# Block means on TensorE and whole rows of keys for the first batch, in a band attention with two gated layers

## The chip, the cores and the metric

One core of a Trainium2 chip runs the kernel. The metric is the device time of one execution in microseconds (us), as a median of several runs. TensorE multiplies matrices, VectorE and ScalarE do element-wise work and reductions, GpSimd does element-wise work too, and SyncE issues the loads. All loads of this kernel stand in SyncE's queue; ScalarE issues the stores and a few copies within on-chip memory.

## The reference

```python
def _attn_ref(q, k, v):                     # 2 batches, 8 heads, 768 rows, 64 columns
    block, window = (32, 16)
    k_sum = k.reshape(B, H, nb, block, D).max(axis=3)
    v_sum = v.reshape(B, H, nb, block, D).mean(axis=3)
    scores_l = scale * np.matmul(q, k.transpose(0, 1, 3, 2))
    mask_l = np.abs(pos[:, None] - pos[None, :]) < window
    scores_s = scale * np.einsum('bhsd,bhnd->bhsn', q, k_sum) + np.log(block)
    scores_all = np.concatenate([np.where(mask_l, scores_l, -1e9), scores_s], axis=-1)
    a = softmax(scores_all)
    return np.matmul(a, np.concatenate([v, v_sum], axis=2))

x = attention as 1536 rows of 512
x = (sigmoid(x @ w_gate) * (x @ w_val)) @ w_out          # 512 -> 1536 -> 512
out = max(x @ w1, x @ w2, x @ w3) @ w_out2               # 512 -> 768 -> 512
```

Each row attends to a band of 31 neighbours and to 24 summaries of blocks of 32 rows: a maximum for the keys, a mean for the values.

## The kernel before

The attention is cut into 16 units: a batch b, a half a of 384 rows, and a pair p of heads. The first eight units are batch 0, units 0 to 3 its first half and units 4 to 7 its second. For one unit, q is loaded with its 128 rows (two heads of 64 columns) on the partitions, and the keys of the unit with the same layout. A tile of 64 queries is scored against 96 neighbouring keys and against the 24 block maxima (L576). VectorE adds the mask and takes the minimum of the negated scores (L583), ScalarE takes exponentials (L589), VectorE normalizes (L594, L595, L598) or, in later units, ScalarE does (L603), TensorE transposes (L608), and a product with the values gives the unit's part of x (L618, "PV").

The keys come in two forms. For units 0 to 3 (`whole`) they are read from `kn`, the whole row of keys of a pair, 768 long with 16 of padding on either side, which is also what the block maxima are taken from (L511). The scores are then two passes, one against windows of `kn` and one against the maxima `ks`. All other units load `kw`, keys laid out in windows of 96 with 24 places behind each; VectorE copies the maxima into these places (L558), and one pass of matmuls does both. There are three buffers for `kn`, two for `kw`, four for `q`, three for `v`.

The block means of v are made once a pair. `vn` holds 96 x 2 x 512 floats: the 32 rows of a block lie on four partitions with eight rows of 64 columns each, for two heads. GpSimd adds the eight rows in three halving steps (L516) into `vr`, one float32 matmul with a constant matrix `avg` adds the four partitions and divides by 32 (L521), ScalarE copies the result out of PSUM (L524) and into the last 24 partitions of the values `vt` (L567, or a DMA at L565 in later units).

The two gated layers behind it use weights that are stored as 64-bit integers; they are loaded in 96 transfers (L392, three buffers `raw`), put together by three VectorE instructions (L399, L404, L408) and split into a high part (ScalarE, L342) and a low part (VectorE, L345). Products with x run in three passes of these parts, 128 x 384 columns a matmul (L697 for the gates and values, L731 for the output product, L821 and L928 in the second layer). The first group of gates and values for batch 0, first half, needs units 0 to 3; its second half needs units 4 to 7.

No engine decides its order while it runs. Each piece of work is a task with an engine, a planned duration, a due time, the tasks it depends on, the buffers it takes and those it uses, and tasks that it must not be planned ahead of (`after`, which orders the plan and adds no wait on the chip). `order` plays the tasks through: for each engine it looks for those that could start first and takes the most pressing by due time, and the instructions are written out in that order. On the chip each engine and the load queue go through this order and wait where something isn't there. Loads are listed as soon as their buffer is free. Until 45 us of the planned time, dummy matmuls on a constant tile (L980) fill TensorE's planned gaps.

Due times of a unit are counted back from its target T: the keys and q by KEYS0 = 14 for units 0 to 3 and KEYS = 24 for others, v by ROWS0 = 2 or ROWS = 4, the rows for the means by SUMS0 = 14 in batch 0 and SUMS = 8 in batch 1.

Of the kernel before, what the change touches and what calls it, by code (L numbers as in the profile page):

```python
# [9 lines left out]
F32 = mybir.dt.float32  # L10
# [30 lines left out]
SLACK = {"PE": 0.05, "DVE": 0.12, "ACT": 0.1, "POOL": 0.0, "SP": 0.0}  # L41
OVER = 0.0
BANKS_H, BANKS_W, BANKS_T = 7, 12, 5
BANKS_KW, BANKS_KN, BANKS_Q, BANKS_V = 2, 3, 4, 3


class Buf:
# [25 lines left out]
class Plan:  # L73
# [11 lines left out]
    def add(self, eng, dur, due, fn, deps=(), new=(), uses=(), after=(), tab=None):  # L85
        t = Task(eng, dur, due, fn, [d for d in deps if d], list(new), list(uses), [d for d in after if d], tab)
        self.tasks.append(t)
        return t
# [114 lines left out]
def kernel(  # L203
# [15 lines left out]
    nc = tc.nc  # L219
    B, NPAIR, _, S = qt.shape  # L220
    D = vw.shape[-1]
    NT, DM = out.shape
    NB = S // BLK
    HALF = S // 2
# [6 lines left out]
    CW = 96 + NB  # L231
# [5 lines left out]
    const = ctx.enter_context(tc.tile_pool(name="const", bufs=1))  # L237
# [7 lines left out]
    ps_m = ctx.enter_context(tc.tile_pool(name="ps_m", bufs=4, space=bass.MemoryType.PSUM))  # L245
    ps_s = ctx.enter_context(tc.tile_pool(name="ps_s", bufs=4, space=bass.MemoryType.PSUM))

    ident = const.tile([128, 128], F32, name="ident")
    masks = const.tile([128, 3, CW], F32, name="masks")
    avg = const.tile([96, 128], F32, name="avg")  # L250

    def build_consts():
        make_identity(nc, ident)
# [27 lines left out]
    add = plan.add  # L281
# [5 lines left out]
    def psum_s(shape):  # L287
        return Buf(ps_s, shape, F32, "s", 4)
# [31 lines left out]
    at = FIRST  # L320
# [152 lines left out]

    att_cm = tc.tile_pool(name="ap", bufs=2)
    ap_ = att_cm.__enter__()
    xt = {(b, a, k): Buf(xp, [128, 2, 2, HALF], F32R, "x", 8) for b in range(B) for a in range(2) for k in range(2)}
    xready = {}
    chain = {}  # L480
# [1 line left out]
    def after(tag, t):  # L482

        p = chain.get(tag)
        if p:
            t.after.append(p)
        chain[tag] = t
        return t

    def load_task(tag, n, shape, src, dur, t):  # L490
        b = Buf(ap_, shape, F32, tag, n)

        def fn(what=tag):
            nc.sync.dma_start(out=b.t[0:src.shape[0]], in_=src)

        return b, after(tag, add("SP", dur, t, fn, new=[b]))

    kblock, vblock = {}, {}
    attention = []

    def make_sums(b, p, T):

        kt, lk = load_task("kn", BANKS_KN, [128, S + 2 * WIN], kn[b, p], 1.14, T - (KEYS if b else KEYS0))
        r, lr = load_task("vn", 2, [96, 2, 8 * D], vn[b, p], 1.092, T - (SUMS if b else SUMS0))
        ks = Buf(ap_, [128, NB], F32, "ks", 4)
        vr = Buf(ap_, [96, 2, D], F32, "vr", 2)
        vs = Buf(ap_, [128, 2 * D], F32, "vs", 4)
        ps = psum_s([128, 2 * D])

        def kmax():  # L510
            nc.vector.tensor_reduce(  # L511
                out=ks.t, in_=kt.t[:, WIN:WIN + S].rearrange("p (n w) -> p n w", w=BLK), axis=AX.X, op=ALU.max)

        def vadd():
            for n in (4, 2, 1):
                nc.gpsimd.tensor_tensor(  # L516
                    out=r.t[:, :, 0:n * D] if n > 1 else vr.t, in0=r.t[:, :, 0:n * D],
                    in1=r.t[:, :, n * D:2 * n * D], op=ALU.add)

        def vmean():  # L520
            nc.tensor.matmul(ps.t, lhsT=avg, rhs=vr.t, start=True, stop=True)  # L521

        def vcopy():
            nc.scalar.activation(out=vs.t, in_=ps.t, func=ACTF.Copy)  # L524

        k = add("DVE", 0.87, T - 13.5, kmax, [lk], [ks], [kt])
        v1 = add("POOL", 2.5, T - 8, vadd, [lr, built], [vr], [r])
        v2 = add("PE", 0.22, T - 5, vmean, [v1], [ps], [vr])
        v3 = add("ACT", 0.2, T - 4.5, vcopy, [v2], [vs], [ps])
        kblock[b, p] = ks, k, kt, lk  # L530
        vblock[b, p] = vs, v3
        attention.extend([k, v1, v2, v3])

    def make_unit(u, i):
        b, p, a = u
        T = target[u]
        if a == 0:
            make_sums(b, p, T)
        whole = i < NPAIR
        ks, kk, kt, lk = kblock[b, p]  # L540
        if not whole:
            kt, lk = load_task("kw", BANKS_KW, [128, TPU, 2, CW], kw[b, p, a], 1.024, T - KEYS)
        q, lq = load_task("q", BANKS_Q, [128, HALF], qt[b, p, :, HALF * a:HALF * a + HALF], 0.546,
                          T - (KEYS0 if whole else KEYS))
        vt, lv = load_task("v", BANKS_V, [CW, TPU, 2, 2, D], vw[b, p, a], 0.82, T - (ROWS0 if whole else ROWS))
# [4 lines left out]
        ps = [psum_s([128, TPU, CW]) for h in range(2)]  # L550
        pa = [(psum_m if i < FREE_M else psum_s)([128, TPU, 128]) for h in range(2)]
        at = [Buf(ap_, [128, TPU, 128], F32, "at", 2) for h in range(2)]
        px = psum_s([128, HALF])
# [7 lines left out]
        def vfill(dma):  # L561
            o = vt.t[96:CW].rearrange("p t par h d -> p (t par) (h d)")
            src = vs.t[96:CW, None, :].to_broadcast([NB, 2 * TPU, 2 * D])
            if dma:
                nc.scalar.dma_start(out=o, in_=src)  # L565
            else:
                nc.scalar.activation(out=o, in_=src, func=ACTF.Copy)  # L567

        def scores(c0, c1):
            for t in range(TPU):  # L570
                for h in range(2):
                    r = slice(64 * h, 64 * h + 64)
                    for par in range(2):
                        c = 128 * t + 64 * par
                        k = kt.t[r, t, par] if not whole else ks.t[r] if c0 else kt.t[r, c:c + 96]
                        nc.tensor.matmul(  # L576
                            ps[h].t[64 * par:64 * par + 64, t, c0:c1], lhsT=q.t[r, c:c + 64], rhs=k,
                            start=True, stop=True)
# [49 lines left out]
        if whole:  # L628
            s0 = after("S", add("PE", 1.25, T - 11, lambda: scores(0, 96), [lk, lq], ps + e + [nm, sm], [q, kt]))
            s1 = add("PE", 0.95, T - 11, lambda: scores(96, CW), [s0, kk], [], [q, ks] + ps)  # L630
            s0.rows, s1.rows = 0.5, 0.25
            attention.append(s0)
        else:
            f1 = add("DVE", 0.23, T - 11.5, fill, [kk, lk], [], [kt, ks])
            s1 = after("S", add("PE", 1.5, T - 11, lambda: scores(0, CW), [f1, lq], ps + e + [nm, sm], [q, kt]))
            s1.rows = 0.45
            attention.append(f1)
        AT = []
# [18 lines left out]
        dma = i >= BY_DMA  # L657
        g1 = add("ACT", 0.12 if dma else 0.83, T - 5, lambda: vfill(dma), [kv], [], [vt, vs], [lv])
        g1.dma = 0.63 if dma else 0.0
        w1 = after("PV", add("PE", 0.95, T, pv, AT + [g1, lv], [px], [vt] + at))  # L660
        key = b, a, p // 2
        first = key not in xstart
        x1 = add("ACT", 0.37, T + 1, xhi, [w1], [x] if first else [], [px] if first else [px, x])
# [279 lines left out]
    built = add("POOL", 5.0, -100.0, build_consts)  # L943
    for i, u in enumerate(units):
        make_unit(u, i)
# [22 lines left out]
    with tc.manual_schedule():  # L968
        idle = const.tile([128, 384], BF16, name="idle")
        nc.vector.memset(idle, 0.0)  # L970
        for t in plan.order():
            for b in t.new:
                b.take()
            if t.idle:
# [3 lines left out]
                n = min(o.shape[1], 384)  # L978
# [62 lines left out]
```

## Time and profile before

| | us |
|---|---|
| median of three runs | 569.16 (568.2 to 570.3) |
| the profiled execution | 567.5 |
| its span, first to last instruction | 565.7 |
| TensorE busy | 545.6 (96%) |
| VectorE busy | 436.3 (77%) |
| ScalarE busy | 291.2 (51%) |
| GpSimd busy | 26.7 (5%) |

The profile is of one execution; its own time stands beside its span, and a median of runs is another number. PE is TensorE's matmuls, PEld its weight loads, DVE VectorE, ACT ScalarE, POOL GpSimd, SPq the load queue. A float32 matmul appears as two records. Busy times of TensorE are of a pipeline, so that a busy engine can still be slow; PEclk is the share of full clock that it was granted.

### The profile page before, as it was taken

What the parts mean: (1) busy time and instruction counts of PE and PEld (TensorE: products, weight loads), DVE (VectorE), ACT (ScalarE), POOL (GpSimd) and SP (SyncE); (2) the same over time, 40 slices, a digit from 0 to 9 for tenths busy, and PEclk for the clock granted to TensorE, in tenths of its full rate; (3) what the DMA queues carried; (4) which work ended last, traced back from release to release, by engine and by line L of the source; (5) the groups of instructions that cost most, each with busy time, mean ns of one, the idle gap of its engine ahead of it and who ended that gap; (6) DMA issues with size and microseconds to landing.
All of it is one profiled execution on the core that took longest, in us unless ns stands there. A gap on an engine that the chain in (4) does not pass through costs nothing.

```text
span 565.7 us, 9849 instructions
## 1 busy us (share of the span) xinstructions
PE 545.6 (96%) x3740; PEld 518.5 (92%) x3740; DVE 436.3 (77%) x995; ACT 291.2 (51%) x665; POOL 26.7 (5%) x42
## 2 busy tenths in 40 slices
PE   7798889999999999999999999999999999999997
PEld 4587779999999999999999999999999999997886
DVE  6998796896897488949996997799999997885000
ACT  3777778678656656966441432435434333453111
POOL 5223300000000000000000000000000000000000
PEclk7979889999999999999999999999999999999999
DMA  8999964565274343520552453130322222000111
GB/s 280 326 259 265 265 206 132 146 229 171 92 235 145 100 106 134 183 80 1 153 193 103 148 158 141 43 108 5 111 82 102 75 75 80 34 0 38 56 75 56
DMA packets 24862, 73.40 MB, mean 130 GB/s; under 512 B 2800, under 2 KB 6256, under 8 KB 24816
## 3 DMA queue, kind: packets, MB, share of 16 engines
q1 hardware_dynamic: 21696, 69.05, 40.4%
q10 hardware_dynamic: 3120, 3.74, 1.9%
q8 instruction: 29, 0.48, 0.3%
q14 instruction: 17, 0.14, 0.1%
HBM read 69.04 MB, written 3.15 MB: 128 GB/s over the span
## 4 chain that ended last, share of the span: by engine, by line
PE 84%; DMA 8%; DVE 5%; ACT 2%; issue 0%; SPq 0%; ACTq 0%; DVEq 0%
PE m L697 31%; PE m L731 17%; PE s L821 11%; PE m L821 11%; PE m L928 9%; DMA raw<-in_wts_dram 4%; DMA kn<-in_kn_dram 3%; DMA v<-in_vw_dram 2%; PE s L618 1%; PE s L608 1%; PE s L576 1%; DVE c L408 1%; DVE c L404 1%; DVE w L345 1%; DVE e L598 0%
## 5 line engine op out<-in xcount | busy, mean ns | idle before, releaser
L697 PE MATMUL m<-x,w 128*128 128x384 f32 x1152 | 212.4, 340 | 0.3 <-ACT t L711 0.3
L697 PEld LDWEIGHTS m<-x,w 128*128 128x128 f32 x1152 | 200.8, 190 | 2.1 <-ACT t L711 0.6
L731 PE MATMUL m<-h,w 128*128 128x384 f32 x576 | 109.1, 341 | 2.4 <-DVE w L345 1.0
L731 PEld LDWEIGHTS m<-h,w 128*128 128x128 f32 x576 | 100.6, 190 | 3.9 <-DVE w L345 1.3
L342 ACT ACTIVATE w<-c 128x512 fp32r<-128x512 f32 x96 | 58.0, 611 | 67.2 <-DVE c L408 43.0
L345 DVE TENSOR_TENSOR w<-c,w 128x512 fp32r<-128x512 f32 x96 | 65.4, 682 | 6.3 <-ACT w L342 6.0
L404 DVE SCALAR_TENSOR_TENSOR c<-raw,c 128x512 int32<-128x512 int32 x96 | 66.3, 691 | 0.6
L408 DVE SCALAR_TENSOR_TENSOR c<-raw,c 128x512 int32<-128x512 int32 x96 | 65.4, 684 | 0.6
L821 PE MATMUL m<-x,w 128*128 128x384 f32 x294 | 56.3, 335 | 1.2 <-ACT t L836 1.2
L821 PE MATMUL s<-f,w 128*128 128x384 f32 x294 | 55.9, 334 | 0.0
L821 PEld LDWEIGHTS m<-x,w 128*128 128x128 f32 x294 | 51.3, 188 | 1.6 <-ACT t L836 1.5
L821 PEld LDWEIGHTS s<-f,w 128*128 128x128 f32 x294 | 51.4, 188 | 0.0
L399 DVE TENSOR_SCALAR c<-raw 128x512 int32<-128x512 int32 x96 | 42.1, 440 | 9.4 <-DMA raw<-in_wts_dram 8.6
L342 ACT ACTIVATE h<-t 128x384 fp32r<-128x384 f32 x48 | 25.0, 522 | 30.5 <-DVE t L716 30.2
L716 DVE TENSOR_TENSOR t<-m,t 128x384 f32<-128x384 f32 x48 | 26.6, 554 | 17.2 <-PE m L697 8.6
L711 ACT ACTIVATE t<-m 128x384 f32<-128x384 f32 x48 | 23.5, 491 | 28.6 <-PE m L697 28.1
L589 ACT ACTIVATE e<-e,nm 128x120 f32<-128x120 f32 x96 | 36.7, 386 | 0.2
L345 DVE TENSOR_TENSOR h<-t,h 128x384 fp32r<-128x384 f32 x48 | 27.5, 576 | 6.7 <-ACT h L342 6.7
L938 ACT ACTIVATE c<-m 128x512 f32<-128x512 f32 (+1 forms) x13 | 7.4, 566 | 40.0 <-PE m L928 39.6
L836 ACT ACTIVATE t<-s 128x384 f32<-128x384 f32 x27 | 13.3, 491 | 24.4 <-PE s L821 24.4
L928 PE MATMUL m<-w,x 128*128 128x512 f32 (+1 forms) x126 | 24.9, 359 | 0.0
L928 PE MATMUL m<-w,f 128*128 128x512 f32 x108 | 24.7, 389 | 0.0
(106 smaller groups left out, 597.2 us busy)
## 6 DMA issues: line engine op xcount, KB each, us to landing
raw<-in_wts_dram SPq DMA_DIRECT2D x96, 512.0 KB, 3.8
v<-in_vw_dram SPq DMA_DIRECT2D x16, 288.0 KB, 4.9
kw<-in_kw_dram SPq DMA_DIRECT2D x12, 360.0 KB, 8.7
kn<-in_kn_dram SPq DMA_DIRECT2D x8, 400.0 KB, 8.8
vn<-in_vn_dram SPq DMA_DIRECT2D x8, 384.0 KB, 9.8
q<-in_qt_dram SPq DMA_DIRECT2D x16, 192.0 KB, 6.3
out_dram<-c ACTq DMA_DIRECT2D x11, 256.0 KB, 2.0
v<-vs ACTq DMA_DIRECT2D x8, 72.0 KB
```

The source lines that it names most:

```text
L342: nc.scalar.activation(out=dst, in_=src, func=ACTF.Copy)
L345: nc.vector.tensor_tensor(out=dst, in0=src, in1=h.bitcast(F32), op=ALU.subtract)
L399: nc.vector.tensor_scalar(out=c.t, in0=half(r, 1), scalar1=5, scalar2=2, op0=ALU.logical_shift_left, op1=ALU.logical_shift_right)
L404: nc.vector.scalar_tensor_tensor(out=c.t, in0=half(r, 1), scalar=-0x40000000, in1=c.t, op0=ALU.bitwise_and, op1=ALU.bitwise_or)
L408: nc.vector.scalar_tensor_tensor(out=c.t, in0=half(r, 0), scalar=29, in1=c.t, op0=ALU.logical_shift_right, op1=ALU.bitwise_or)
L589: nc.scalar.activation(out=e[h].t[:, t], in_=e[h].t[:, t], func=ACTF.Exp, scale=-1.0, bias=nm.t[:, h, t:t + 1], accum_out=sm.t[:, h, t:t + 1])
L697: nc.tensor.matmul(ps.t, lhsT=w.t.rearrange("p s (k f) -> p s k f", k=KC)[:, wh, kc], rhs=src[kc // 2].t[:, xh, kc % 2], start=(kc == 0 an ...
L711: k1 = after("t", add("ACT", 0.371, end, lambda: nc.scalar.activation(out=s.t, in_=ps.t, func=ACTF.Sigmoid), [l], [s], [ps], tab="S"))
L716: k2 = after("t", add("DVE", 0.469, end, lambda: nc.vector.tensor_tensor(out=t.t, in0=ps2.t, in1=s.t, op=ALU.mult), [l2, k1], [t], [ps2, s]))
L731: nc.tensor.matmul(ps.t, lhsT=w.t.rearrange("p s (k f) -> p s k f", k=KC)[:, wh, dm], rhs=h.t[:, xh], start=(i == 0 and j == 0), stop=(i = ...
L821: nc.tensor.matmul(ps.t, lhsT=w.t[:, wh, c:c + 128], rhs=x.t[:, xh, kc], start=new and n == 0, stop=n == 5, skip_group_check=True)
L928: nc.tensor.matmul(ps.t[:, c0:c1], lhsT=h.t[:, xh, e, c:c + 128], rhs=w.t[:, wh, c0:c1], start=(f == 0 and i == 0), stop=(f == NF2 - 1 and ...
```

## The change

For batch 0, GpSimd's additions go. `vsum` multiplies `avg` with each of the eight rows of `vn` and accumulates the eight products in the same PSUM tile. Batch 1 keeps the additions, and its load of `vn` for pair p is planned behind the PV product of unit 4 + p. `whole` now holds for all of batch 0, so that units 4 to 7 read windows out of `kn` at an offset, with no `kw` load and no copies; their q and v take the due times of whole units. `kn` has four buffers instead of three, `q` three instead of four. The constants `ident`, `masks` and `avg` lie in the pool of the attention, which is opened earlier and is given back when the attention has ended.

```diff
-BANKS_KW, BANKS_KN, BANKS_Q, BANKS_V = 2, 3, 4, 3
+BANKS_KW, BANKS_KN, BANKS_Q, BANKS_V = 2, 4, 3, 3
...
-    ident = const.tile([128, 128], F32, name="ident")
-    masks = const.tile([128, 3, CW], F32, name="masks")
-    avg = const.tile([96, 128], F32, name="avg")
+    att_cm = tc.tile_pool(name="ap", bufs=2)
+    ap_ = att_cm.__enter__()
+
+    def constant(name, shape):
+        return ap_.tile(shape, F32, name=name, tag=name, bufs=1)
+
+    ident = constant("ident", [128, 128])
+    masks = constant("masks", [128, 3, CW])
+    avg = constant("avg", [96, 128])
...
-    kblock, vblock = {}, {}
+    kblock, vblock, pvs = {}, {}, {}
...
-        vr = Buf(ap_, [96, 2, D], F32, "vr", 2)
...
+        def vsum():
+
+            for n in range(8):
+                nc.tensor.matmul(
+                    ps.t, lhsT=avg, rhs=r.t[:, :, D * n:D * n + D], start=(n == 0), stop=(n == 7))
...
-        v1 = add("POOL", 2.5, T - 8, vadd, [lr, built], [vr], [r])
-        v2 = add("PE", 0.22, T - 5, vmean, [v1], [ps], [vr])
+        if b == 0:
+            v1, v2 = None, add("PE", 1.75, T - 5, vsum, [lr, built], [ps], [r])
+        else:
+            lr.after.append(pvs[4 + p])
+            vr = Buf(ap_, [96, 2, D], F32, "vr", 2)
+            v1 = add("POOL", 2.5, T - 8, vadd, [lr, built], [vr], [r])
+            v2 = add("PE", 0.22, T - 5, vmean, [v1], [ps], [vr])
...
-        whole = i < NPAIR
+        whole = b == 0
...
-                        k = kt.t[r, t, par] if not whole else ks.t[r] if c0 else kt.t[r, c:c + 96]
+                        k = kt.t[r, t, par] if not whole else ks.t[r] if c0 else kt.t[r, HALF * a + c:HALF * a + c + 96]
...
-        w1 = after("PV", add("PE", 0.95, T, pv, AT + [g1, lv], [px], [vt] + at))
+        pvs[i] = w1 = after("PV", add("PE", 0.95, T, pv, AT + [g1, lv], [px], [vt] + at))
```

## Rows read from the trace of the kernel before

**Rows 1.** Busy time by stretch; "(x)" is the number of instructions:
```profile
core 0: us, PE busy (x) PEld busy (x) DVE busy (x) ACT busy (x) POOL busy (x), PEclk, DMA share, GB/s
0.00:72.75 72.75, 58.23 (x627) 46.95 (x627) 60.62 (x186) 48.97 (x141) 26.73 (x42) 0.88 0.99 278
72.75:565.70 492.95, 487.34 (x3114) 471.51 (x3114) 375.70 (x810) 242.22 (x524) 0.00 (x0) 1.00 0.34 108
```

**Rows 2.** The chain that ended last: start, duration, what:
```profile
41.36 10.68 DMA raw<-in_wts_dram
...
57.97 11.66 DMA raw<-in_wts_dram
...
72.75 3.46 PE m L731 x10
```

**Rows 3.** Dummies' busy time (L980 alone); TensorE group L608: busy, mean ns | idle, releaser:
```profile
0.00:72.75 72.75, 11.39 (x46) 5.75 (x46) 0.88 0.99 278
...
L608 PE MATMUL s<-ident,e 128*120 128x128 f32 x24 | 4.9, 329 | 6.1 <-DVE e L598 6.1
```

**Rows 4.** VectorE groups, 0 to 72.75 us, shapes apart:
```profile
L399 DVE TENSOR_SCALAR c<-raw 128x512 int32<-128x512 int32 x12 | 6.8, 565 | 8.6 <-DMA raw<-in_wts_dram 8.6
...
L558 DVE COPY kw<-ks 128x72 f32<-128x72 f32 x6 | 0.9, 194 | 0.0
```

**Rows 5.** VectorE's timeline: start, duration, instruction:
```profile
8.13 1.26 DVE L345 TENSOR_TENSOR w<-c,w 128x512 fp32r<-128x512 f32 x1 [0.70 <-ACT w L342]
...
26.73 1.59 DVE L598 TENSOR_TENSOR e<-e,sm 128x360 f32<-128x360 f32 x1
...
35.70 0.42 DVE L594 TENSOR_SCALAR sm<-sm 128x3 f32<-128x3 f32 x1
...
44.07 1.68 DVE L345 TENSOR_TENSOR w<-c,w 128x512 fp32r<-128x512 f32 x1
...
71.15 0.94 DVE L404 SCALAR_TENSOR_TENSOR c<-raw,c 128x512 int32<-128x512 int32 x1
```

**Rows 6.** Durations of single lines, whole execution: ns min/median/max, first and last start:
```profile
L345 DVE TENSOR_TENSOR w<-c,w x96: 416/684/1679, 8.1 to 494.0; 128x512 fp32r<-128x512 f32 x87, 128x256 fp32r<-128x256 f32 x9
...
L399 DVE TENSOR_SCALAR c<-raw x96: 396/422/948, 4.5 to 486.8; 128x512 int32<-128x512 int32 x96
...
L598 DVE TENSOR_TENSOR e<-e,sm x12: 523/526/1595, 15.7 to 58.3; 128x360 f32<-128x360 f32 x12
...
L594 DVE TENSOR_SCALAR sm<-sm x20: 152/165/778, 13.9 to 243.9; 128x6 f32<-128x6 f32 x12, 128x3 f32<-128x3 f32 x8
```

**Rows 7.** GpSimd's timeline, third and fourth pair of batch 0:
```profile
26.50 2.41 POOL L516 TENSOR_TENSOR vn<-vn 96x512 f32<-96x512 f32 x2 [10.45 <-DMA vn<-in_vn_dram]
...
28.98 0.45 POOL L516 TENSOR_TENSOR vr<-vn 96x128 f32<-96x128 f32 x1
...
32.84 2.49 POOL L516 TENSOR_TENSOR vn<-vn 96x512 f32<-96x512 f32 x2 [3.41 <-DMA vn<-in_vn_dram]
```

**Rows 8.** TensorE's timeline: scores, means, one product:
```profile
7.86 1.12 PE L576 MATMUL s<-kn,q 64*64 64x96 f32 x24 [1.92 <-DMA q<-in_qt_dram]
...
25.50 0.72 PE L576 MATMUL s<-kn,q 64*64 64x96 f32 x24
26.04 0.50 PE L576 MATMUL s<-ks,q 64*64 64x24 f32 x24
...
36.81 0.39 PE L521 MATMUL s<-vr,avg 96*128 96x128 f32 x2
...
40.41 0.85 PE L576 MATMUL s<-kw,q 64*64 64x120 f32 x24
...
62.92 0.92 PE L618 MATMUL s<-at,v 120*64 120x64 f32 x24
...
67.25 0.61 PE L521 MATMUL s<-vr,avg 96*128 96x128 f32 x4
```

**Rows 9.** Loads of `vn`, from issue to landing:
```profile
DMA to landing us min/median/max: 5.7/9.8/11.2
```

More of the change, by code (lines that the diff above doesn't have):

```diff
@@ L472, in blocks @@
             wready["P", nm, f, name] = k
-    att_cm = tc.tile_pool(name="ap", bufs=2)
-    ap_ = att_cm.__enter__()
     xt = {(b, a, k): Buf(xp, [128, 2, 2, HALF], F32R, "x", 8) for b in range(B) for a in range(2) for k in range(2)}
@@ L531, in make_sums @@
         vblock[b, p] = vs, v3
-        attention.extend([k, v1, v2, v3])
+        attention.extend([k, v2, v3] + ([v1] if b else []))
     def make_unit(u, i):
```

## The prediction

> **What bounds the kernel now.** I read the busy times by stretch first [rows 1]. From 72.75 us to the end TensorE is busy for 487.34 of 492.95 us; before that for 58.23 of 72.75 us, at a mean granted clock of 0.88 (a mixture of its two levels, 2.4 and 1.2 GHz). So the kernel is a TensorE stream with a start-up of some 73 us ahead of it, and TensorE is not what limits that start-up. The DMA engines are: their share is 0.99 of the 72.75 us, at 278 GB/s, which makes 20.2 MB. VectorE is next with 60.62 us busy.
>
> The chain of waits says the same [rows 2]. Two weight transfers of 10.68 and 11.66 us stand in it, and at 72.75 us TensorE takes it over. What shortens the start-up therefore arrives at the end in full, as long as it adds nothing to TensorE's work behind 72.75 us. What TensorE does within the start-up has cover: its busy time includes 11.39 us of dummy matmuls that compute nothing, and its transposes (L608) wait 6.1 us for VectorE's L598 [rows 3].
>
> VectorE's groups of the start-up show where its time goes [rows 4]: it waits 8.6 us for weights at L399, and L399 takes 565 ns in the mean there. Over the whole execution the same instruction has a median of 422 ns [rows 6]. Its timeline [rows 5] beside that of GpSimd [rows 7] gives the reason: the stretched instructions lie under GpSimd's additions of v rows. L345 takes 1.26 us instead of 0.684, L598 1.59 instead of 0.526, L594 0.42 instead of 0.165 [rows 5, 6]. In the first batch ten instructions are stretched so, from the one at 8.13 to the one at 35.70 us, by 4.9 us together; under the second batch's additions nine, from 44.07 to 71.15 us, by 3.9 us.
>
> **The change, part by part.** I count in the start-up, by VectorE's time and waits, then let TensorE take its part back.
>
> (1) First batch's additions leave GpSimd: VectorE gets the 4.9 us back. Lower bound 0, if the instructions only wait elsewhere; upper bound the whole time of the additions, 2.41 + 0.45 = 2.86 us a pair [rows 7], 11.4 us for four. I take 4.9, since VectorE is busy or waiting for weights nearly throughout. The Trainium skill (SBUF — State Buffer, "Who interferes with whom") says that a VectorE instruction with two SBUF inputs and a GpSimd instruction that reads SBUF exclude each other, the later one blocking fully. [...]
>
> (2) The means become eight matmuls a pair. One mean takes 0.39 us in two records, two in a row 0.61 us in four [rows 8], so a further one costs 0.22 us: 0.39 + 7 x 0.22 = 1.9 us, against 0.39 before, 1.5 more a pair and 6.0 for four. The first two pairs fall where the dummies run, and replace them: nothing. Without that cover they cost 3.0. The other two fall behind 23 us, where TensorE has gaps, but the gaps will shrink; I charge them in full, 3.0 us.
>
> (3) Units 4 to 7 score against whole rows of k, in two passes: 0.72 + 0.50 us instead of one of 0.85 [rows 8], 0.37 more each. Three of them in the start-up make 1.1 us on TensorE; the fourth lies behind 72.75 us and costs 0.4 there, uncovered. VectorE drops two copies a unit, 0.9 us for the six in the start-up [rows 4]. Bounds 0 and 0.9; I take 0.9.
>
> (4) Bytes. The four window loads go, 128 x 720 floats each, 1.47 MB. The second batch's rows for the means (96 x 1024 floats, 0.39 MB each) are now listed behind the P V product of units 4 to 7. Unit 5's stands at 62.92 us [rows 8], so two of the four, 0.79 MB, leave the start-up. The second batch's whole rows of k come later too, since four of the first batch hold their buffers until units 4 to 7 have scored; I count nothing for those, they still fall into the start-up or shortly behind it. At 278 GB/s, 2.26 MB are 8.1 us of a queue that is full. VectorE's wait for weights is 8.6 us [rows 4]. Lower bound 0 (the three weight buffers set the pace anyway), upper 8.1; I take half, 4.0, since the transfers in front of a weight load are only partly those that go. By the 358 GB/s that the Trainium skill gives for HBM transfers (SBUF — State Buffer, "Summary: rules for kernel authors") the 2.26 MB would be 6.3 us and the term 3.2; the rows have 278 at a share of 0.99, and the measurement decides.
>
> (5) With two of the second batch's loads, their additions leave the start-up too: half of 3.9 us, 2.0. Behind 72.75 us they are covered: VectorE is busy there for 375.70 of 492.95 us [rows 1]. Without the cover they come back, 2.0.
>
> (6) The constants move to the attention's memory, and the loads of q and v of units 4 to 7 get later due times, with one buffer of q less. No instruction is added. What could be late is q: the first scores of the kernel stand 1.92 us for it [rows 8], and the same wait once more would cost 1.9. A gain is excluded, since the bytes are counted in (4). Between 0 and 1.9 I take 0, as the scores of units 3 and 5 [rows 8] stand without a wait.
>
> Sum: -4.9 - 0.9 - 4.0 - 2.0 = -11.8; TensorE takes back 3.0 + 1.1 + 0.4 = 4.5. Net -7.3. Check by bytes alone: (20.2 - 2.26) MB at 278 GB/s are 64.5 us, 8.2 less than 72.75. The two agree within a microsecond. The profiled execution took 567.5 us, so 560.2; its span is 565.7, 1.8 us less. The median of the three runs shown is 1.7 us higher, so the forecast for a median is 561.9, say 562. With (1) and (4) at half or at their bounds the same case runs from 557 to 566.
>
> **The rivals.**
>
> *The start-up shrinks until TensorE fills it.* Real work in it is 58.23 - 11.39 = 46.8 us [rows 1, 3], part of it at half clock; the change adds 7.1, which makes 54 us. Half clock costs 0.12 x 72.75 = 8.7 us at most [rows 1]; I take off half of it, 4, as the rest lies under dummies and gaps. From the first scores at 7.86 us [rows 8] the start-up then ends near 58, 14.5 us sooner, and with the 0.4 the time is 553.4, median 555. For it: VectorE's 60.62 us [rows 1] less the 7.8 of (1), (3) and (5) are 52.8, which fits in 58. Against: the order on each engine is fixed, and the 6.1 us of gaps before the transposes [rows 3] don't vanish all at once.
>
> *Nothing comes of it.* The weights keep their pace: three buffers, two conversions in hand, about 11 us from issue to landing [rows 2]. Then what VectorE gains it waits for at L399, and TensorE's 4.5 us eat the rest: the first batch's 4.9 and the copies' 0.9 less 4.5, -1.3, so 566.2, median 567.9. For it: L399's 8.6 us show that the weights are already late. Against: the bytes in front of them shrink.
>
> *The second batch's means come too late, and it is slower.* Their loads are issued later, and where the order written ahead expects a load to land sooner than it does, the mean stands too early in TensorE's queue; from issue to landing the trace has 5.7 at the least, 9.8 in the median [rows 9]. TensorE takes its queue in order, so a mean that isn't ready stops the large product behind it, now inside the stretch where nothing covers it. Price: 9.8 - 5.7 = 4.1 us a pair, 16.4 for four: 567.5 - 7.3 + 16.4 = 576.6, median 578. From 10.1 us of such stalls on, three pairs of the four, the kernel is slower than before. Against: two of these means stand in the queue at 67.25 us [rows 8], behind the product of unit 5 and before those of units 6 and 7, far ahead of the units that need them, so there is room to move them back.
>
> **How the numbers follow.** Chances: the forecast 0.58, TensorE-filled 0.13, nothing 0.15, late means 0.14. A measurement of this kernel tells about 0.5% from no change, 2.8 us: a median below 566.3 is faster, one above 572.0 slower. Of the forecast's own 0.58 I put 0.02 inside those bounds. Of "nothing", whose median of 567.9 lies 1.6 us inside the lower one, 0.04 below them, 0.10 inside and 0.01 above; of the late means 0.02 inside, when only one or two pairs stall, and 0.02 below. Faster: 0.56 + 0.13 + 0.04 + 0.02, 0.75. Same: 0.02 + 0.10 + 0.02, 0.14. Slower: 0.01 + 0.10, 0.11. The range takes in the TensorE-filled case (555, less a microsecond) and "nothing" (568, plus one): 554 to 569.
>
> **What would show it.** Right: GpSimd's additions for four pairs of heads instead of eight, no stretched VectorE instruction before some 45 us, the lasting TensorE stretch beginning at 64 to 67 us, L399's waits near 4 us, 64 records of means on TensorE for the first batch in place of 8. Term (4) is wrong if those waits stay near 8.6 us; (2) if TensorE waits for rows of v before a mean; (6) if it waits for q. The whole is wrong if a gap of several microseconds appears behind the start-up, before a mean of the second batch.

## The result

| | median, us | runs | ratio to before, 95% interval |
|---|---|---|---|
| before | 569.16 (568.2 to 571.17) | 5 | |
| changed | 564.06 (563.75 to 565.39) | 5 | 0.991 [0.9885, 0.9935] |

In this timing the changed kernel is 5.1 us faster; 7.2 were forecast. Timed once more, beside the last experiments, it took 564.67 us in 12 runs against 567.15 in 35 of the kernel before, a ratio of 0.9969 [0.9938, 1.0001]. That is 1.8 us by the ratio and 2.5 by the medians, and the interval just reaches no change. What differs between the two timings is the kernel before: its runs there went from 562.36 to 570.65, those of the changed one from 563.57 to 566.95. The kernel before was timed in two more sets, for the experiments, with medians of 565.62 and 566.66 us, so the 569.16 of the first timing is the highest of four. A gain is likely, then, but rather of 1 to 3 us than of 5.

The profiled executions are 3.4 us apart, 567.5 and 564.06 us, their spans 565.7 and 562.3. The changed kernel's busy time by stretch, columns as in [rows 1]:

```profile
0.00:72.75 72.75, 60.79 (x869) 54.43 (x869) 62.51 (x207) 53.21 (x158) 10.15 (x24) 1.00 0.88 268
72.75:562.30 489.55, 483.06 (x3058) 466.98 (x3056) 368.23 (x781) 233.62 (x506) 5.96 (x6) 1.00 0.34 107
```

GpSimd's 26.73 us in the first 72.75 us are 10.15, the DMA share fell from 0.99 to 0.88, and the granted clock rose from 0.88 to 1.00. VectorE is as busy as before, with 207 instructions done in this stretch instead of 186. The bytes are 268 GB/s x 72.75 us = 19.5 MB; before they were 20.2. But the changed kernel is further on at 72.75 us, and two more weight loads have been issued by then, 16 instead of 14. The stretches up to the first products of batch 0's second half, before and then changed, end at the same place of the work:

```profile
0.00:80.81 80.81, 66.30 (x702) 54.10 (x703) 68.09 (x214) 54.59 (x161) 26.73 (x42) 0.87 0.95 268
```

```profile
0.00:74.92 74.92, 62.96 (x881) 56.60 (x882) 64.68 (x211) 54.70 (x163) 10.15 (x24) 1.00 0.88 269
```

By these, 21.7 MB became 20.2, 1.5 MB less, about what the four window loads carry.

The chain of waits of the changed kernel, in order of time:

```profile
4.20 8.31 DMA vn<-in_vn_dram
...
14.23 10.56 DMA vn<-in_vn_dram
...
29.93 8.26 DMA raw<-in_wts_dram
...
66.94 2.21 PE m L745 x11
```

The two weight transfers of [rows 2], with loads of k and v ahead of them, gave way to two loads of v rows, which TensorE's means now wait for directly, and one weight transfer. TensorE takes the chain over at 66.94 us instead of 72.75, and loses it once more, from 85.73 to 104.08 us, to VectorE and ScalarE, which is where the second batch's first unit is due.

VectorE's groups of the first 72.75 us, changed kernel; L405, L612 and L572 are the lines that were L399, L598 and L558:

```profile
L405 DVE TENSOR_SCALAR c<-raw 128x512 int32<-128x512 int32 x14 | 7.3, 530 | 4.8 <-DMA raw<-in_wts_dram 4.7
L612 DVE TENSOR_TENSOR e<-e,sm 128x360 f32<-128x360 f32 x12 | 6.2, 525 | 0.0
...
L608 DVE TENSOR_SCALAR sm<-sm 128x3 f32<-128x3 f32 x8 | 1.3, 162 | 0.3 <-ACT e L603 0.3
...
L572 DVE COPY kw<-ks 128x72 f32<-128x72 f32 x3 | 0.5, 191 | 0.0
```

The same two groups in the kernel before:

```profile
L598 DVE TENSOR_TENSOR e<-e,sm 128x360 f32<-128x360 f32 x12 | 7.5, 637 | 0.0
...
L594 DVE TENSOR_SCALAR sm<-sm 128x3 f32<-128x3 f32 x8 | 3.1, 392 | 0.6 <-ACT e L589 0.5
```

L612 and L608 run at the medians of [rows 6], 525 and 162 ns: under the first batch nothing stretches them any more. The wait for weights is 4.8 us where [rows 4] had 8.6. But three copies of L572 stand there, and the first batch needs none. The load queues show where they come from, before and then changed:

```profile
56.40 0.35 SPq L494 DMA_DIRECT2D kw<-in_kw_dram  x1
...
77.13 0.33 SPq L494 DMA_DIRECT2D kw<-in_kw_dram  x1
```

```profile
13.18 0.33 SPq L498 DMA_DIRECT2D kw<-in_kw_dram  x1
14.23 0.78 SPq L498 DMA_DIRECT2D vn<-in_vn_dram  x1
16.89 0.33 SPq L498 DMA_DIRECT2D kw<-in_kw_dram  x1
...
19.70 0.33 SPq L498 DMA_DIRECT2D vn<-in_vn_dram  x1
```

The rows with `kw` are the same two loads in both: the windows of units 8 and 9, of the second batch. Four window loads are gone, and these two moved forward, from 56.40 and 77.13 us to 13.18 and 16.89, because their buffers were free. Of the second batch's four loads of rows for the means, which went out by 53.94 us before, three go out within the 72.75 us and the fourth at 74.49.

Where the gain goes can be read from two marks on TensorE, the same products in both kernels: the first of batch 0's second half, and the first that its first half multiplies with the third and last group of gate and value weights. TensorE's timelines, before and then changed:

```profile
80.81 3.28 PE L697 MATMUL m<-x,w 128*128 128x384 f32 x18
...
166.73 1.55 PE L697 MATMUL m<-x,w 128*128 128x384 f32 x8
```

```profile
24.83 2.05 PE L520 MATMUL s<-vn,avg 96*128 96x128 f32 x16 [1.07 <-DMA vn<-in_vn_dram]
...
74.92 1.21 PE L711 MATMUL m<-x,w 128*128 128x384 f32 x6
...
163.30 1.89 PE L711 MATMUL m<-x,w 128*128 128x384 f32 x10
```

The start-up is 5.9 us shorter (80.81 to 74.92). At the second mark 3.4 are left, and they stay to the end. A second profile of the changed kernel (564.99 us) has the marks at 75.98 and 163.90 us, so 4.8 and 2.8 us. Between the marks, by stretch, before and then changed:

```profile
80.81:166.73 85.92, 85.92 (x650) 82.85 (x649) 70.12 (x179) 59.05 (x138) 0.00 (x0) 1.00 0.52 163
```

```profile
74.92:163.30 88.38, 87.54 (x655) 83.30 (x655) 64.06 (x166) 54.05 (x131) 5.96 (x6) 1.00 0.45 146
```

The stretch is 2.5 us longer. 0.84 us of it are idle TensorE, where it had none before. Three means of the second batch, which stood in the start-up before, lie in it now, as the changed kernel's TensorE group of this stretch and its timeline show:

```profile
L530 PE MATMUL s<-vr,avg 96*128 96x128 f32 x6 | 1.2, 273 | 0.0
```

```profile
96.44 0.39 PE L530 MATMUL s<-vr,avg 96*128 96x128 f32 x2
96.58 2.34 PE L745 MATMUL m<-h,w 128*128 128x384 f32 x12
```

They are busy for 1.2 us, but that overlaps with their neighbours: the next product starts 0.14 us behind each. So they take some 0.4 us of the stretch, and the other 1.2 us are spread over products and transposes that follow each other a little more slowly, for which no single cause was found.

### The profile page after: what moved, and what is told of

Its sections match the earlier page's. It is cut to its first block, busy times and chain, and to the rows that moved or that the text cites. A ratio compares the mean times of both kernels' runs of the same rounds, so it can differ in the third digit from the quotient of the medians.

```text
span 562.3 us, 10192 instructions
## 1 busy us (share of the span) xinstructions
PE 543.9 (97%) x3924; PEld 521.4 (93%) x3924; DVE 430.7 (77%) x987; ACT 286.8 (51%) x663; POOL 16.1 (3%) x30
## 4 chain that ended last, share of the span: by engine, by line
PE 81%; DVE 7%; DMA 5%; ACT 5%; issue 1%; SPq 1%; ACTq 0%; DVEq 0%
PE m L711 30%; PE m L745 16%; PE s L835 11%; PE m L835 11%; PE m L942 9%; DMA vn<-in_vn_dram 3%; PE s L632 2%; DMA raw<-in_wts_dram 1%; DVE c L414 1%; DVE c L410 1%; PE s L622 1%; ACT e L617 1%; ACT e L603 1%; DVE c L405 1%; PE s L590 1%
## 5 line engine op out<-in xcount | busy, mean ns | idle before, releaser
L745 PE MATMUL m<-h,w 128*128 128x384 f32 x576 | 107.3, 338 | 0.7 <-DVE h L351 0.7
L745 PEld LDWEIGHTS m<-h,w 128*128 128x128 f32 x576 | 99.3, 188 | 2.0 <-DVE h L351 1.4
L351 DVE TENSOR_TENSOR w<-c,w 128x512 fp32r<-128x512 f32 x96 | 63.8, 665 | 12.6 <-ACT w L348 12.4
L405 DVE TENSOR_SCALAR c<-raw 128x512 int32<-128x512 int32 x96 | 41.7, 437 | 5.7 <-DMA raw<-in_wts_dram 4.7
```

Source lines behind the costliest of these rows:

```text
L351: nc.vector.tensor_tensor(out=dst, in0=src, in1=h.bitcast(F32), op=ALU.subtract)
L405: nc.vector.tensor_scalar(out=c.t, in0=half(r, 1), scalar1=5, scalar2=2, op0=ALU.logical_shift_left, op1=ALU.logical_shift_right)
L745: nc.tensor.matmul(ps.t, lhsT=w.t.rearrange("p s (k f) -> p s k f", k=KC)[:, wh, dm], rhs=h.t[:, xh], start=(i == 0 and j == 0), stop=(i = ...
```

## The experiments

The theories: what counts is VectorE's time under GpSimd's additions (VectorE theory), the bytes in the load queue (byte theory), TensorE's clock (clock theory), or VectorE and the queue together, each hiding the other's relief (two-limits theory, formed after the first eight runs). "M" are the means by eight matmuls, "K" the keys of units 4 to 7 from whole rows with the buffers that go with it, "R" the second batch's rows planned late. The first four kernels were timed beside one set of runs of the kernel before (565.62 us), the next four beside another (566.66), the last four beside a third (567.15), each set on a chip of its own. So ratios of different sets can differ by the scatter of the kernel before, whose medians are up to 0.3% apart.

**M alone**, onto the kernel before, with `vsum` as in the change:

```diff
...
+        if b == 0:
+            v1, v2 = None, add("PE", 1.75, T - 5, vsum, [lr, built], [ps], [r])
+        else:
             vr = Buf(ap_, [96, 2, D], F32, "vr", 2)
             v1 = add("POOL", 2.5, T - 8, vadd, [lr, built], [vr], [r])
             v2 = add("PE", 0.22, T - 5, vmean, [v1], [ps], [vr])
...
```

> Of the change only the means of batch 0 by eight matmuls; keys, loads and buffers as before. VectorE theory (what counts is that the additions no longer block VectorE): -4.9 us for the stretched instructions, +3.0 for the matmuls, about -2 against before. Byte theory (what counts is the loads that leave the start-up): no load leaves, so +3. Clock theory (what counts is that the eight matmuls keep TensorE's clock at 2.4 GHz where before shows four stretches at a granted clock of 0.50): -4 to -5, and the stretches at 0.50 are gone.

574.07 us, 1.0154 [1.0118, 1.0191]: slower than any theory said. VectorE's group, the first 72.75 us by stretch, and the chain:

```profile
L607 DVE TENSOR_TENSOR e<-e,sm 128x360 f32<-128x360 f32 x12 | 6.2, 525 | 0.0
L399 DVE TENSOR_SCALAR c<-raw 128x512 int32<-128x512 int32 x12 | 5.1, 426 | 11.9 <-DMA raw<-in_wts_dram 11.9
```

```profile
0.00:72.75 72.75, 55.25 (x667) 49.51 (x667) 53.91 (x178) 43.57 (x122) 13.04 (x28) 0.91 0.98 278
```

```profile
11.46 9.84 DMA raw<-in_wts_dram
...
38.40 11.79 DMA raw<-in_wts_dram
...
53.17 10.77 DMA raw<-in_wts_dram
```

L607 runs clean at 525 ns, VectorE's busy time fell from 60.62 to 53.91 us, and its wait for weights rose from 8.6 to 11.9. The queue is as full as before (0.98, 278 GB/s). Half of VectorE's freed time turned into waiting for weights; it also did less in this stretch, 178 instructions instead of 186. That TensorE's added work makes up the rest of the loss was not shown.

**K alone**: the changed kernel with GpSimd's additions for all pairs and without the line of R.

```diff
-        if b == 0:
-            v1, v2 = None, add("PE", 1.75, T - 5, vsum, [lr, built], [ps], [r])
-        else:
-            lr.after.append(pvs[4 + p])
-            ...
+        vr = Buf(ap_, [96, 2, D], F32, "vr", 2)
+        v1 = add("POOL", 2.5, T - 8, vadd, [lr, built], [vr], [r])
+        v2 = add("PE", 0.22, T - 5, vmean, [v1], [ps], [vr])
...
```

> Of the change only the keys of units 4 to 7 from whole rows, with four key buffers, three of q and the constants in the attention's pool; GpSimd still adds for all pairs and the second batch's rows are loaded as before. VectorE theory: -0.9 for the copies, +1.5 for the second pass of scores, about +0.6. Byte theory: 1.47 of the 2.26 MB go, -2.6 us of waits, +1.5, about -1; VectorE's wait for weights falls from 8.6 to about 6. Clock theory: the stretches at 0.50 stay, no gain.

570.94 us, 1.009 [1.0062, 1.0118]. VectorE's wait for weights fell to 6.4 us, as the byte theory said, but the time rose. The queue of this kernel has the two window loads of units 8 and 9 at 13.72 us and all four row loads of the second batch between 30 and 47 us, where they went out between 33 and 54 before: as above, later loads moved forward.

**R alone**, onto the kernel before:

```diff
+        if b == 1:
+            lr.after.append(pvs[4 + p])
...
```

> Of the change only that the second batch's rows for the means are planned behind the PV products of units 4 to 7. VectorE theory: half of the second batch's 3.9 us of stretching leaves the start-up, -2. Byte theory: 0.79 MB leave, -1.4. Clock theory: 0. Late-means rival: slower by 4 us a pair where TensorE waits for a mean.

569.54 us, 1.0053 [1.0026, 1.008]. The wait for weights fell to 5.6 us; the time didn't follow. The late-means rival's price of 4 us a pair isn't there: TensorE waited 2.5 us in all for GpSimd's sums, longest 1.5, against 1.1 before. The profile doesn't hold the loss at all: its execution took 567.71 us, one of the faster of the 12, and has the two marks at 80.71 and 166.85 us, where the kernel before has 80.81 and 166.73.

**TensorE's work alone**: the kernel before, its one matmul eight times, with the scale of the copy and the planned duration to match.

```diff
-            nc.tensor.matmul(ps.t, lhsT=avg, rhs=vr.t, start=True, stop=True)
+            for n in range(8 if b == 0 else 1):
+                nc.tensor.matmul(ps.t, lhsT=avg, rhs=vr.t, start=(n == 0), stop=(n == (7 if b == 0 else 0)))
...
```

> The kernel before, with GpSimd's additions kept, and the one matmul of each mean of batch 0 done eight times on the added rows, the sum scaled by an eighth when it is copied. It has TensorE's added work and nothing else of the change. VectorE theory and byte theory: +3 to +6, the work alone. Clock theory: the added matmuls keep the clock, the stretches at 0.50 shrink, and the time is at most that of before, down to -3.

573.57 us, 1.013 [1.0096, 1.0164]. More work on TensorE didn't hold the clock: the mean granted clock is 0.986 in the median of its runs, 0.989 in those of the kernel before. So the clock theory falls in the form that the eight matmuls by themselves keep the clock. This kernel and M alone differ by what M removes, GpSimd's additions and their stretching, and by the order of their lists, and they take the same time within their intervals: in the start-up as it was, no cost of the additions shows. VectorE's wait for weights in the first 72.75 us of this kernel is

```profile
DVE c L399 <- DMA raw<-in_wts_dram: 4.3, 3, 3.3
```

It is half of the 8.6 us of before, though no load was removed and the kernel is slower. So this wait, which the byte theory goes by, follows neither the bytes in the queue alone nor the time.

**Additions put back** into the changed kernel, onto a tile that nobody reads:

```diff
+            gh = Buf(ap_, [96, 2, D], F32, "vr", 2)
+
+            def spare():
+                for n in (4, 2, 1):
+                    for m in range(n):
+                        nc.gpsimd.tensor_tensor(
+                            out=gh.t, in0=r.t[:, :, m * D:m * D + D], in1=r.t[:, :, (n + m) * D:(n + m) * D + D], op=ALU.add)
+
+            attention.append(add("POOL", 2.5, T - 8, spare, [lr, built], [gh], [r]))
```

> The changed kernel, with GpSimd adding the rows of batch 0 all the same, in seven small additions a pair into a tile that nobody reads. Only the additions' load on VectorE's SBUF accesses comes back. VectorE theory: 4.9 us or a little more come back, ratio about 1.000. Byte theory and clock theory: as the changed kernel, ratio 0.991.

565.61 us, 0.9987 [0.9962, 1.0012]. VectorE's groups of its first 72.75 us (L621 and L617 are L612 and L608 above):

```profile
L621 DVE TENSOR_TENSOR e<-e,sm 128x360 f32<-128x360 f32 x12 | 8.0, 675 | 0.0
...
L617 DVE TENSOR_SCALAR sm<-sm 128x3 f32<-128x3 f32 x8 | 2.3, 290 | 1.7 <-ACT e L612 1.7
```

The stretching is back: 8.0 us for 6.2 and 2.3 for 1.3, 2.8 us in these two groups (0.8 of it in one instruction under the second batch's additions). The time is 4.4 us above the changed kernel's first ratio (0.0077 x 566.66) and 1.0 us above its second (0.0018). The intervals of this kernel and of the second ratio overlap, so a cost isn't shown. If there is one, it needn't be VectorE's: the seven small additions keep a pair's rows in use for some 4.7 us, the eight matmuls for 2.05, and there are two buffers for these rows.

**The changed kernel without R:**

```diff
-            lr.after.append(pvs[4 + p])
```

> The changed kernel without the line that plans the second batch's rows behind the PV products. VectorE theory: the second batch's additions return to the start-up, +2 us (ratio 0.9945). Byte theory: 0.79 MB return, +1.4. Clock theory: 0 (ratio 0.991).

571.17 us, 1.0074 [1.0037, 1.0112]: all of the gain goes and more, and no theory had a loss of this size. The wait for weights is 9.2 us, where the changed kernel has 4.8.

**The window loads put back** into the changed kernel, unread:

```diff
+        if b == 0 and a == 1:
+            load_task("kw", BANKS_KW, [128, TPU, 2, CW], kw[b, p, a], 1.024, T - KEYS)
```

> The changed kernel, with the four window loads of units 4 to 7 issued all the same into buffers that nobody reads. Byte theory: 1.47 MB return to a full queue, +2.6 to +5.3 us (ratio 0.9955 to 1.000). VectorE theory and clock theory: within 1 us of the changed kernel (ratio 0.991).

567.98 us, 1.0029 [1.0009, 1.0049]. The ratio lies above the byte theory's range; against the changed kernel's second ratio the loads cost 3.4 us, within its +2.6 to +5.3, and against the first 6.7, above it. VectorE's waits:

```profile
DVE c L405 <- DMA raw<-in_wts_dram: 9.1, 6, 3.4
```

**Without dummies**, the changed kernel:

```diff
-                if t.new and at < 45.0:
+                if t.new and at < 0.0:
```

> The changed kernel without the dummy matmuls of the start. Clock theory: TensorE runs at 0.50 in parts of the start-up again, +2 to +4 us (ratio 0.9945 to 0.998). VectorE theory and byte theory: TensorE isn't the limit there, within 1 us of the changed kernel.

566.64 us, 1.0006 [0.9984, 1.0028]. TensorE's timeline begins:

```profile
7.96 3.76 PE L520 MATMUL s<-vn,avg 96*128 96x128 f32 x16 [7.96 <-DMA vn<-in_vn_dram]
...
14.15 3.78 PE L520 MATMUL s<-vn,avg 96*128 96x128 f32 x16 [0.68 <-DMA vn<-in_vn_dram]
```

The eight matmuls take 3.76 us instead of 2.05. The dummies are worth 2.1 us against the second ratio, within the clock theory's +2 to +4, and 5.4 against the first, above it; the intervals of this kernel and of the second ratio overlap. The granted clock misleads here. Over the first of these means the profile gives it as 1.00, while a mean of the kernel with two window loads later, below, takes the same time at 0.50:

```profile
7.96:11.70 3.74, 3.74 (x20) 3.52 (x20) 2.79 (x6) 0.00 (x0) 0.00 (x0) 1.00 1.03 365
```

```profile
25.93:29.70 3.77, 3.77 (x17) 3.77 (x18) 2.65 (x7) 0.10 (x2) 0.00 (x0) 0.50 1.05 236
```

By the durations the kernel without dummies ran its first means at 1.2 GHz, and the profile doesn't count it. So the mean clock of its runs, 0.9965 in the median, can't be set beside the 0.995 of the changed kernel.

**The changed kernel again, and the two pairs that were missing.** M with R, K with R, and the changed kernel with two window loads later; the edits of the first two are the lines above.

> The changed kernel itself, timed again beside the other three on one chip, since executions of one kernel scatter by some 4 us either way. All theories: ratio 0.991, and less than 0.995.

564.67 us, 0.9969 [0.9938, 1.0001], above the 0.995 that all theories expected. By the ratio the gain is a third of that in the first timing, and it isn't clear of no change.

> The means by eight matmuls and the second batch's rows planned late; keys as before. Means alone took 1.0154 of before, late rows alone 1.0053. If the parts simply add, 1.021. Two-limits theory (VectorE and the load queue each hold the start-up, so that relief of one shows only when the other is relieved too): the late rows take 0.8 MB and the second batch's additions out of the start-up, so the means' freed VectorE time can show: 1.000 to 1.005, with VectorE's wait for weights below the 11.9 us of means alone. Clock theory: as means alone, 1.015, if the stretches at 0.50 stay.

568.91 us, 1.0042 [1.0005, 1.0079]. The ratio is what the two-limits theory gave, but the sign that it named hardly shows: the wait for weights is 11.1 us, where M alone has 11.9.

> The keys of units 4 to 7 from whole rows and the second batch's rows planned late; GpSimd adds for all pairs. Keys alone took 1.009, late rows alone 1.0053. If the parts add, 1.014. Two-limits theory: bytes are relieved twice but VectorE not at all, so the additions still hold it: about 1.000, no better than the changed kernel with additions put back (0.9987). Byte theory: the queue alone counts, 0.993.

566.73 us, 0.9997 [0.9967, 1.0027], as the two-limits theory said. The wait for weights is 3.4 us, the least of all. Against this kernel the changed one differs by M alone, and is 0.3% faster, within the two intervals.

```diff
             kt, lk = load_task("kw", BANKS_KW, [128, TPU, 2, CW], kw[b, p, a], 1.024, T - KEYS)
+            if a == 0 and p < 2:
+                lk.after.append(pvs[4 + p])
```

> The changed kernel, with the window loads of units 8 and 9, which now stand at 13 and 17 us in the load queue, planned behind the PV products of units 4 and 5. Byte theory and two-limits theory: 0.74 MB leave a full queue ahead of the rows that the third and fourth pair's means wait for, at some 300 GB/s 2.4 us; ratio 0.985 to 0.989. Clock theory and VectorE theory: as the changed kernel, 0.991.

568.19 us, 1.0033 [0.9999, 1.0066]: all theories wrong. TensorE's timeline:

```profile
25.93 3.79 PE L520 MATMUL s<-vn,avg 96*128 96x128 f32 x16 [1.52 <-DMA vn<-in_vn_dram]
...
32.62 2.20 PE L713 MATMUL m<-x,w 128*128 128x384 f32 x9
```

The third pair's mean starts at 25.93 us, in the changed kernel at 24.83: 0.74 MB fewer ahead of its rows didn't bring them sooner (in the changed kernel's second profile it starts at 26.33). The mean runs at half clock, and the first large product stands at 32.62 us instead of 22.61, because the planner wrote TensorE's list in another order. Between the two marks (78.20 and 168.87 us) this kernel takes 90.67 us, the changed one 88.38.

All eight combinations, as ratio to before, with VectorE's wait for weights in one profiled execution each:

| | without R | with R |
|---|---|---|
| neither | 1 / 8.6 us | 1.0053 / 5.6 |
| M | 1.0154 / 11.9 | 1.0042 / 11.1 |
| K | 1.009 / 6.4 | 0.9997 / 3.4 |
| M and K | 1.0074 / 9.2 | 0.9969 / 4.8 (first timing 0.991) |

If the parts added, the three together would cost 1.54 + 0.9 + 0.53 = 3.0%, 17 us; they gain 0.3 to 0.9%. That the parts don't add is clear of the scatter; differences of some 0.3% between the cells are not. R costs 0.5% alone and is worth 0.9 to 1.1% beside M, K or both (by the second timing). M raises the wait for weights wherever it is added, and R lowers it.

## Why the prediction was right, and where it was not

By the first timing the direction, the range and the likeliest case came out. In part that is luck: the five runs of the kernel before in it have the highest median of four sets. By the second timing the gain of 1.8 to 2.5 us lies nearer the 1.3 of "nothing comes of it" than the 7.3 of the sum. The mechanism came out in part: the start-up shrinks, by 5.9 and 4.8 us in two profiles, but its parts don't add as the sum has them. By its steps:

- **(1), 4.9 us back for VectorE.** The instructions did get clean (L612 7.5 to 6.2 us, L608 3.1 to 1.3). That VectorE's time turns into the kernel's time was assumed, and no run shows it: with M alone a part of it became waiting for weights, which is the mechanism of the rival "nothing comes of it", and beside K and R, M gains 0.3%, within the intervals. Put back into the changed kernel, the additions cost 1.0 to 4.4 us, the lower not clear of noise.
- **(2), 1.9 us a pair** was 2.05. The first two pairs replaced dummies, and the work alone, in the kernel before, cost 1.3% of 565.62, 7.4 us, where the uncovered price was to be 6.0. The prediction's sign for a wrong (2) appeared: TensorE waited for rows of v before three means, 2.5 us together, which the step doesn't price:

```profile
PE s L520 <- DMA vn<-in_vn_dram: 2.5, 3, 1.1
```

- **(3)** was right for the scores, 0.72 or 0.73 and 0.49 us a unit. Of the copies 0.4 us went, not 0.9, as those of units 8 and 9 came forward.
- **(4)** had the right size: the wait for weights fell by 3.8 us against 4.0. But that wait is no measure of the bytes, as the kernel with TensorE's work alone shows (4.3 us with every load in place). Of the 2.26 MB, 0.7 left the first 72.75 us, and 1.5 the stretch up to the first mark: the windows went, the rows of the second batch hardly did. That two later windows move forward the prediction didn't see, though a load is listed as soon as its buffer is free. Put back, the four loads nearly double the wait (9.1 us), as the step said.
- **(5)** held for GpSimd, which adds two of four pairs in the start-up. Its cover was looked for on VectorE alone. TensorE's means of the second batch moved behind the start-up with them.
- **(6)** held: TensorE waited for q once, 1.2 us, less than the 1.9 of before. A wait for q was to be the sign of a wrong (6), but the kernel before has one too.
- **The sum.** The step that failed is that what shortens the start-up "arrives at the end in full", less the only cost put behind it, "the fourth costs 0.4 there, uncovered". The fourth unit's scores stand at 64.05 us in the changed kernel, still in the start-up. Behind it 2.5 us were lost for which the sum has no term: 0.84 idle, some 0.4 for three means, the rest spread. The start-up's -5.9 and these +2.5 make the profile's -3.4, against -7.7 and +0.4. The ends of "557 to 566" don't come from the bounds of (1) and (4): with both at half the median is 566, with both at their bounds it runs from 551 to 571.

The rival of late means didn't come at its price of 4.1 us a pair. TensorE's waits from 72 to 180 us in the changed kernel are these; none stands before a mean, and one, 0.5 us, is for the copy of a mean into the values (`v<-vs`):

```profile
PE s L632 <- DMA v<-vs: 0.5, 1, 0.5
PE s L632 <- ACT y L761: 0.3, 1, 0.3
PE m L745 <- DVE h L351: 0.3, 1, 0.3
PE s L632 <- issue: 0.3, 1, 0.3
```

What stays open is the cause of the gain. No theory had all the results right, and it isn't known why R alone and K alone are slower, although VectorE waits less for weights in both. Each edit also gives another order of every engine's list, and no run here holds the order fixed while the work changes; the kernel with two window loads later shows that such a reordering can move the first product by 10 us. How much of each single ratio is order and how much is the edit wasn't separated. TensorE's clock, in the last section, isn't excluded either.

## What to carry to other kernels

A load queue that issues whatever has a free buffer brings later loads forward when loads are removed: look which ones will move. Holding loads back can pay or cost. Beside the other parts, it gained about 1% with the second batch's rows and lost 0.6% with two window loads, so time it. Parts of a change that each look like a gain can each be a loss until all of them are in; time them together before dropping one. A gain that depends on which runs of the kernel before it is set beside needs more of these runs. Mark the same instruction in both traces at several places along the span: the gain at the end of the first stage isn't the gain at the end.

## What the runs showed of the hardware

The granted clock of the start-up rose from 0.88 to 1.00, for which the sum has no term. The page's row of 40 slices, before and then changed:

```profile
PEclk7979889999999999999999999999999999999999
```

```profile
PEclk9999999999999999999999999999999999999999
```

In pieces of 5 us, the kernel before was granted 0.51 from 10 to 15 us, 0.50 from 30 to 35, 0.73 from 60 to 65 and 0.79 from 70 to 75, so it was at 1.2 GHz for all or a part of each. In the 5 us ahead of the second and third piece TensorE had been busy for 2.64 of 5 and, from 55 to 60, for 1.56. In the changed kernel's first profile the clock doesn't fall once in the start-up; in its second it is 0.83 from 20 to 30 us, and the first mark comes 1.1 us later. The price of the low level can be read from eight matmuls of the means, 3.79 us at 1.2 GHz and 2.05 at 2.4. Over 30 runs of the kernel before, the mean clock lay between 0.981 and 0.991 and the time between 571.18 and 563.88 us, with a correlation of -0.54: a run whose clock is better by 0.01 is 3.4 us shorter in a straight-line fit. The median mean clock is 0.997 and 0.995 in the changed kernel's two timings and 0.987 to 0.989 in the kernel before, which by that fit would be 2 to 3.4 us, about as much as the gain. Whether the clock is the cause or only goes with fewer waits no run here separates: eight matmuls alone don't bring it, and without the dummies no gain shows (1.0006).
